# The first head's row of shifts: spread on TensorE and copied in, where a transfer carried it

## The chip, the cores and the metric

One Trainium2 chip, one of its cores. The metric is the device time of one execution, in microseconds (us), median over runs. TensorE (PE) does products, with its own queue for loading weights (PEld); VectorE (DVE) and ScalarE (ACT) do elementwise work and reductions; GpSimd (POOL) does elementwise work; SyncE (SP) issues most transfers (DMAs). Each engine works its instructions in the order in which the program lists them.

## What is computed

Attention over 4 batches x 8 heads, 768 tokens, 64 dimensions, in which a query sees only the keys of its own hash bucket (six sign bits of a projection), followed by a soft mixture of experts. Cut to what matters here:

```python
q_bits = (np.einsum('bhsd,dk->bhsk', q, proj) > 0)
k_bits = (np.einsum('bhsd,dk->bhsk', k, proj) > 0)
mask = q_bucket[:, :, :, None] == k_bucket[:, :, None, :]
scores = np.where(mask, scale * np.matmul(q, k.transpose(0, 1, 3, 2)), -1e9)
scores = scores - np.max(scores, axis=-1, keepdims=True)
attn = np.exp(scores)
attn = attn / (np.sum(attn, axis=-1, keepdims=True) + 1e-09)
x = attn @ v                     # all heads, to (3072, 512)
logits = x @ phi                 # 8 experts x 4 slots
slot_out = relu(softmax(logits, tokens).T @ x @ w1) @ w2
return softmax(logits, slots) @ slot_out
```

## The kernel before, in words

**One head.** For a head, tile Y holds in its 128 partitions the high parts of q (side 0) and k (side 1) in rows 0 to 63, one row (64) for a shift, twelve rows of sign bits scaled so that any mismatch costs a huge penalty, and low parts in rows 96 to 127; tile X holds the other parts of the split. Three pairs of X and Y go round (`XYs`, `N_Y` = 3), so that head 0 has the first pair, head 1 the second, head 2 the third. `smax` (line 463) makes approximate masked scores with rows 0 to 95 of Y, queries in the output's partitions, and VectorE takes the maximum of each query (lines 477 and 480). A head's 6 x 768 columns of maxima products lie in nine tiles of 512 columns (some products have 512, some 256), in two PSUM buffers; each tile has one reduction. `shift` (line 484) turns the maxima into the shifts of the 768 queries (three small VectorE operations, lines 489 to 492): `mz` holds in columns 0 to 5 minus the maximum of query tile t, and in columns 6 to 11 a large number for queries with no match. `shift_rows` (line 496) must lay these as a row over the 768 queries into partition 64 of side 0, the first six into X and the others into Y: TensorE transposes `mz` (line 499), ScalarE copies the 12 x 128 result to SBUF (line 502), and SyncE moves it with one transfer into the row (line 503, through `move`, line 383). `scores` (line 506) then makes the exact scores with keys in the output's partitions, two products for each piece (Y first, X second), again nine tiles of 512 columns, here in three PSUM buffers, and ScalarE takes the exponential (line 519) into `pts`. `av` (line 534, products on line 544) multiplies them with the values, `acc` (GpSimd, lines 526 and 532) sums them.

**Order.** Nothing is scheduled by a tool: `STEADY` and `ONCE` (lines 45 to 155) give each step of each head a due time, in units of one slot, `at` (line 894) looks it up, and the steps are sorted by it (line 983) and listed in that order. Steps without a line of their own take that of the steady pattern. Negative times are the start, before the steady pattern. So the tables fix the order in every engine's queue, and the times in them are ranks, not microseconds.

**The start.** Head 0 is treated apart. Its bits come from `first_bits` (products, line 437; query and key, each in two pieces, each piece in its own group of 32 output partitions), and `first_over` (line 426) compares them on VectorE straight into Y (`over`, line 409). Bits of later heads are made by `bits` (line 418, products on line 415), compared into the tile `bt`, and moved from there into Y by four transfers a head (`spread_bits`, line 453). `more_bits` (line 444) makes head 1's bits. `load_cst` (line 289) loads the identity, which `copy_ident` (line 340, on GpSimd) copies where TensorE uses it. `spin` (line 326) runs products on a tile of ones, `idle`, only to keep TensorE going; `smax` of head 0 runs one after most of its products (line 482). `idle` lies in the third X tile, and `first_rows(2)` (line 343, on GpSimd) fills that tile and the third Y tile's rows later: lines 346, 347 and 348. `load(4)` (line 258) fetches q and k of heads 4 and 5.

**Around the change** TensorE's list is, before the change: the transpose of head 0's shifts, two maxima products of head 1, `spin(2)`, four more maxima products, then the first scores of head 0, mixed with the remaining maxima of head 1; then, head 0's last scores mixed with head 2's first maxima, among them the transpose of head 1's shifts; then head 0's `av`. SyncE's list is: the row of head 0's shifts, `load(4)`, head 2's four bit transfers, the values of head 1 (`load_v`), `spread_x(1)` and `spread_l(2)`, the row of head 1's shifts.

```python
    def first_rows(i):
        ts = XYs[i] if i else Xs[0]
        if i == 2:
            nc.gpsimd.memset(Xs[2][64:96, 0].bitcast(F32), 0.0)
        nc.gpsimd.memset((ts[64:96, 1] if i == 2 else ts[64:96]).bitcast(F32), 0.0)
        nc.gpsimd.memset(ts[ROW:ROW + 1, 1].bitcast(F32), 1.0)
```

`one_rec` (line 645), near the kernel's end, already does the kind of product that the change adds: a column of a tile, broadcast to 32 columns as weights, times the identity (line 650), two columns for each of three ranges, in two groups of output partitions.

## Time and profile before

| | |
|---|---|
| median of 3 runs | 469.77 us (469.76 to 470.04) |
| the profiled execution's own time | 471.7 us |
| its span, first to last instruction | 469.8 us |
| granted TensorE clock, mean of the span | 0.998 |
| TensorE busy | 458.1 us, 98% |
| VectorE busy | 388.7 us, 83% |
| ScalarE busy | 247.9 us, 53% |
| GpSimd busy | 327.2 us, 70% |

How to read it: the profile is of one execution. Its times count from the start of the span. A row of a timeline gives start, duration, engine, line of the program, operation, output<-inputs, shapes and how many instructions were merged into the row, and in square brackets the idle time of the engine ahead of it with what ended it; "issue" is time in which the engine waited for nothing that the profile shows. A merged row's duration runs from the first start to the last end. Products are pipelined, so that one may start before the record of the one ahead has ended; TensorE's pace is read from the distance of starts, or from the chain. A product of plain float32 numbers is counted as two instructions. The chain is the work that ended last, followed back from the last instruction.

### The profile page before, as it was taken

Reading aid. Unit: us, or ns where it says so; the run is one execution under the profiler, and the core shown is the slowest. Engines: PE = TensorE matmul, PEld = TensorE weight load, DVE = VectorE, ACT = ScalarE, POOL = GpSimd, SP = SyncE. Lnnn points to the kernel's source line nnn. Section 1 sums busy time; section 2 is a strip of 40 time slices with the busy share of each in tenths; the row PEclk is TensorE's granted clock in tenths of the full one; section 3 lists DMA queues with packets and bytes.
Section 4 is the critical chain, followed back from the end, with each engine's and each line's share of the span. In section 5 each row is a group of like instructions: output and inputs, shape, how many; then the busy total and the mean of one; then the engine's idle time right before and its main releaser. Section 6 shows DMA issues by size and latency. Waiting matters only on the chain.

```text
span 469.8 us, 10650 instructions
## 1 busy us (share of the span) xinstructions
PE 458.1 (98%) x3974; PEld 289.6 (62%) x3974; DVE 388.7 (83%) x722; ACT 247.9 (53%) x469; POOL 327.2 (70%) x205
## 2 busy tenths in 40 slices
PE   8989999999999999999999999999999999999993
PEld 3556666667666666666656666666666666554472
DVE  6848898989888898989898979898888987777953
ACT  5255646464656655555555464646566546541242
POOL 7867977878785988787868988787849888910000
PEclk9999999999999999999999999999999999999999
DMA  5757578868686677868684877775756669999997
GB/s 156 182 146 176 152 159 239 170 196 193 186 203 170 136 185 178 232 173 228 165 224 136 190 220 168 231 169 171 179 187 145 197 162 299 340 355 367 411 357 315
DMA packets 39792, 99.24 MB, mean 211 GB/s; under 512 B 7471, under 2 KB 13757, under 8 KB 39741
## 3 DMA queue, kind: packets, MB, share of 16 engines
q1 hardware_dynamic: 39580, 98.17, 73.8%
q8 instruction: 31, 0.51, 0.5%
q10 hardware_dynamic: 160, 0.39, 0.4%
q14 instruction: 21, 0.16, 0.1%
HBM read 52.71 MB, written 6.29 MB: 126 GB/s over the span
## 4 chain that ended last, share of the span: by engine, by line
PE 92%; DVE 1%; issue 1%; POOL 0%; ACT 0%; DVEq 0%
PE st L515 29%; PE av L544 26%; PE smx L474 16%; PE mi L1101 3%; PE qh L1051 3%; PE mi L556 2%; PE mi L415 2%; PE mi L607 2%; PE mi L572 2%; PE mi L592 1%; PE mi L788 1%; PE mi L499 1%; PE qh L1121 1%; PE qa L1065 0%; POOL stage L379 0%
## 5 line engine op out<-in xcount | busy, mean ns | idle before, releaser
L519 ACT ACTIVATE pt<-st 128x512 f32<-128x512 f32 x288 | 164.0, 596 | 62.6 <-PE st L515 56.9
L515 PE MATMUL st<-XY 128*128 128x256 f32 (+1 forms) x768 | 177.8, 347 | 0.0
L532 POOL TENSOR_TENSOR acc<-acc,pt 128x768 f32<-128x768 f32 x85 | 155.8, 1833 | 6.5
L480 DVE TENSOR_REDUCE mx<-smx 128x1 f32<-128x512 f32 x192 | 131.0, 688 | 26.9 <-PE smx L474 24.4
L515 PEld LDWEIGHTS st<-XY 128*128 128x128 f32 x768 | 125.2, 190 | 17.6 <-ACT pt L519 1.7
L474 PE MATMUL smx<-XY 96*128 96x512 f32 (+1 forms) x384 | 119.2, 359 | 1.7 <-issue 1.3
L474 PEld LDWEIGHTS smx<-XY 96*128 96x128 f32 x384 | 66.7, 190 | 31.4 <-issue 11.5
L532 POOL TENSOR_TENSOR av<-av,pt 128x768 f32<-128x768 f32 x40 | 73.4, 1836 | 3.1
L477 DVE TENSOR_REDUCE mx<-smx 128x2 f32<-128x512 f32 x96 | 65.8, 686 | 5.2 <-PE smx L474 4.5
L544 PE MATMUL av<-pt,av 128*32 128x384 f32 x768 | 67.6, 486 | 0.0
L526 POOL TENSOR_TENSOR acc<-pt 128x768 f32<-128x768 f32 x22 | 40.4, 1838 | 37.4 <-ACT pt L519 37.4
L544 PE MATMUL av<-pt,v 128*32 128x384 f32 x768 | 65.5, 486 | 0.0
L548 ACT COPY avs<-av 128x384 f32<-128x384 f32 x32 | 15.2, 476 | 83.9 <-PE av L544 83.9
L376 DVE TENSOR_REDUCE stage<-stage 128x768 fp32r<-128x1536 f32 x28 | 49.2, 1790 | 0.0
L564 DVE RECIPROCAL dl<-sm 128x128 f32<-128x128 f32 x45 | 38.8, 916 | 12.1 <-ACT sm L559 8.3
L544 PEld LDWEIGHTS av<-pt,av 128*32 128x32 f32 x768 | 24.9, 110 | 36.8 <-issue 36.4
L544 PEld LDWEIGHTS av<-pt,v 128*32 128x32 f32 x768 | 24.9, 110 | 36.0 <-issue 35.2
L526 POOL TENSOR_TENSOR av<-pt 128x768 f32<-128x768 f32 x10 | 18.4, 1838 | 15.5 <-ACT pt L519 15.5
L369 ACT ACTIVATE stage<-stage 128x768 fp32r<-128x768 f32 x28 | 22.5, 836 | 4.4 <-DMA stage<-qk 2.1
L609 DVE TENSOR_TENSOR xq<-mi,r 128x256 f32<-128x256 f32 x45 | 17.4, 415 | 1.1 <-PE mi L607 1.1
L880 DVE STREAM_TRANSPOSE w<-call 32x256 f32<-32x256 f32 (+2 forms) x48 | 14.9, 333 | 1.6 <-PE qh L1051 1.1
L1101 PE MATMUL mi<-w 128*32 128x128 f32 (+1 forms) x336 | 15.1, 299 | 0.0
(209 smaller groups left out, 401.7 us busy)
## 6 DMA issues: line engine op xcount, KB each, us to landing
w<-w SPq DMA_DIRECT2D x51, 512.0 KB
XY<-stage SPq DMA_DIRECT2D x62, 384.0 KB
XY<-stage SPq DMA_DIRECT2D x62, 192.0 KB
stage<-qk SPq DMA_DIRECT2D x28, 384.0 KB
out<-stage SPq DMA_DIRECT2D x12, 512.0 KB
stage<-w SPq DMA_DIRECT2D x7, 512.0 KB
av<-vt SPq DMA_DIRECT2D x16, 192.0 KB
v<-vt SPq DMA_DIRECT2D x16, 192.0 KB
```

What stands on the lines that cost most here:

```text
L369: nc.scalar.activation(w[:, 2 * x], raws(h, x), AF.Copy, scale=-1.0 if h > 2 else 1.0)
L376: nc.vector.tensor_reduce(out=w[:, 2 * x + 1], in_=stage[:, x:n + 1:n - x].rearrange("p t s -> p s t"), axis=AX.X, op=ALU.add, negate=True)
L474: nc.tensor.matmul(pt[:, o:o + b - a], Ys[h % N_Y][0:96, 0, t * P:(t + 1) * P], Ys[h % N_Y][0:96, 1, a:b], start=True, stop=True)
L477: nc.vector.tensor_reduce(out=mx[:, n - 1:n + 1], in_=pt.rearrange("p (a x) -> p a x", a=2), axis=AX.X, op=ALU.max)
L480: nc.vector.reduce_max(out=mx[:, n:n + 1], in_=pt, axis=AX.X)
L515: nc.tensor.matmul(pt[:, o:o + b - a], x[:, 1, i * P:(i + 1) * P], x[:, 0, a:b], start=first, stop=not first)
L519: nc.scalar.activation(pts[i // 2][:, 512 * u:512 * u + 512], pt, AF.Exp, scale=D ** -0.5)
L526: nc.gpsimd.tensor_tensor(out=s["acc"], in0=pr[:, 0:S], in1=pr[:, S:2 * S], op=ALU.add)
L532: eng.tensor_tensor(out=s["acc"], in0=s["acc"], in1=pr[:, a * S:(a + 1) * S], op=ALU.add)
L544: nc.tensor.matmul(s["av"][D * c + d:D * c + d + 32, 0:HC], s["v"][:, i, d:d + 32], pr[:, o + c * HC:o + (c + 1) * HC], start=(i == 0), st ...
L564: nc.vector.reciprocal(out=st[h]["rs"][:, k * P:(k + 1) * P], in_=st[h]["sm"][:, k * P:(k + 1) * P])
L1101: nc.tensor.matmul(po[32 * j:32 * j + 32], hTs[g][:, f, 32 * j:32 * j + 32], wt[1, x, 2 * g + f // 4, j][f % 4][:, cols], start=(g + f == ...
```

## The change

For head 0 alone, `shift_rows` no longer transposes and moves. Instead `first_shift` multiplies each column of `mz`, broadcast to 32 columns as weights, with the identity: 12 products of 128 columns, in three ranges of columns (k) by four groups of 32 output partitions (j). After them, partition 0 of each group holds half a row (384 queries): groups 0 and 1 the halves of X's row, groups 2 and 3 those of Y's. Two copies on ScalarE (X) and two on VectorE (Y) put them into partition 64, half 1 first. Head 1 and later keep the transfer.

The due times change: in TensorE's list, two idle products (`spin(2)`) now follow the first score products, and not head 1's second maxima product; after them head 0's score products alternate with head 1's maxima from the start; all of head 0's scores and the transpose of head 1's shifts come ahead of head 2's first maxima. The list from head 0's shifts on, for each step (head, tile, part):

```
before: shift_rows 0, smax 1,1,1  1,3,1, spin 2, smax 1,0,1  1,1,0  1,5,1  1,2,0, scores 0,2,1  0,3,0,
  smax 1,2,1  1,3,0, scores 0,0,1  0,1,0, smax 1,4,1  1,5,0, scores 0,4,0, smax 1,4,0, scores 0,3,1,
  smax 1,0,0, scores 0,1,1  0,2,0, shift 1, scores 0,0,0  0,4,1, smax 2,0,0, scores 0,5,0, smax 2,0,1,
  shift_rows 1, smax 2,1,0, scores 0,5,1, smax 2,3,1, av 0
after: shift_rows 0, smax 1,1,1  1,3,1, scores 0,2,1  0,3,0, spin 2, smax 1,0,1  1,1,0, scores 0,0,1  0,1,0,
  smax 1,5,1, scores 0,4,0, smax 1,2,0, scores 0,3,1, smax 1,2,1  1,3,0, scores 0,1,1, smax 1,4,1  1,5,0,
  scores 0,2,0, smax 1,4,0, scores 0,0,0, smax 1,0,0, shift 1, scores 0,4,1  0,5,0  0,5,1, shift_rows 1,
  smax 2,0,0  2,0,1  2,1,0  2,3,1, av 0
```

`first_rows(2)`, `load(4)` and `spread_bits(2)` keep their place behind `spin(2)` in the list. Besides, head 0's bits are made and compared in halves of 384 columns, four compares and not five, all ahead of the first maxima product; and the identity's load is listed right behind head 0's values.

```diff
-    ('first_over', 0, 0, 256): -110.0, ('first_over', 0, 256, 512): -100.0, ('first_over', 0, 512, 768): -99.0,
-    ('first_over', 1, 0, 512): -111.0, ('first_over', 1, 512, 768): -109.0, ('first_rows', 0): -115.0,
+    ('first_over', 0, 0, 384): -110.0, ('first_over', 0, 384, 768): -109.0, ('first_over', 1, 0, 384): -111.0,
+    ('first_over', 1, 384, 768): -110.5, ('first_rows', 0): -115.0,
...
-    ('load_cst',): -104.0, ('load_room', 0): 183.9, ('load_room', 1): 184.93, ('load_room', 2): 184.94,
+    ('load_cst',): -112.9, ('load_room', 0): 183.9, ('load_room', 1): 184.93, ('load_room', 2): 184.94,
...
-    ('scores', 0, 0, 0): 0.919282, ('scores', 0, 0, 1): -10.094785, ('scores', 0, 1, 0): -7.0839,
-    ('scores', 0, 1, 1): 0.473768, ('scores', 0, 2, 0): 0.521698, ('scores', 0, 2, 1): -13.756044,
-    ('scores', 0, 3, 0): -13.67708, ('scores', 0, 3, 1): -1.029943, ('scores', 0, 4, 0): -4.991552,
-    ('scores', 0, 4, 1): 1.039496, ('scores', 0, 5, 0): 1.620748, ('scores', 0, 5, 1): 3.699083,
+    ('scores', 0, 0, 0): -0.7, ('scores', 0, 0, 1): -19.2, ('scores', 0, 1, 0): -19.1,
+    ('scores', 0, 1, 1): -9.0, ('scores', 0, 2, 0): -3.0, ('scores', 0, 2, 1): -29.0,
+    ('scores', 0, 3, 0): -28.9, ('scores', 0, 3, 1): -14.0, ('scores', 0, 4, 0): -17.0,
+    ('scores', 0, 4, 1): 1.039496, ('scores', 0, 5, 0): 1.3, ('scores', 0, 5, 1): 1.4,
...
-    ('shift_rows', 1): 2.323009, ('shift_rows', 2): 11.070264, ('smax', 0, 0, 0): -101.0, ('smax', 0, 0, 1): -98.0,
+    ('shift_rows', 1): 1.45, ('shift_rows', 2): 11.070264, ('smax', 0, 0, 0): -101.0, ('smax', 0, 0, 1): -98.0,
...
     def first_over(x, a, b):
-        j = 2 * x + a // 512
-        over(Ys[0][64:80, x, a:b], first_pt[x], slice(32 * j, 32 * j + 16), cols=slice(a % 512, a % 512 + b - a))
+        j = 2 * x + a // HC
+        over(Ys[0][64:80, x, a:b], first_pt[x], slice(32 * j, 32 * j + 16), cols=slice(a % HC, a % HC + b - a))
...
-        for c, (a, b) in enumerate(((0, 512), (512, S))):
+        for c, (a, b) in enumerate(((0, HC), (HC, S))):
...
         pt = s["mt"]
+        if h == 0:
+            first_shift(pt, s["mz"])
+            return
         nc.tensor.transpose(pt[:, 0:P], s["mz"], ident)
...
+    def first_shift(pt, mz):
+        for k in range(3):
+            for j in range(4):
+                nc.tensor.matmul(pt[32 * j:32 * j + 32, k * P:(k + 1) * P],
+                                 mz[:, 3 * j + k:3 * j + k + 1].broadcast_to([P, 32]), ident, start=True, stop=True)
+        row = XYs[0][ROW:ROW + 1, 0].rearrange("o y (c s) -> o (y c) s", c=2)
+        for j in (1, 0):
+            nc.scalar.copy(row[:, j], pt[32 * j:32 * j + 1, 0:HC])
+            nc.vector.tensor_copy(row[:, 2 + j], pt[64 + 32 * j:64 + 32 * j + 1, 0:HC])
...
-    for xab in ((1, 0, 512), (0, 0, 256), (1, 512, S), (0, 256, 512), (0, 512, S)):
+    for xab in ((1, 0, HC), (1, HC, S), (0, 0, HC), (0, HC, S)):
         at(first_over, *xab)
```

## Rows read from the trace of the kernel before

**Rows 1.** The page's chain that ended last, shares of the span by engine.

```profile
PE 92%; DVE 1%; issue 1%; POOL 0%; ACT 0%; DVEq 0%
```

**Rows 2.** Waits of TensorE, whole span: who waited for whom, total, times, longest.

```profile
PE smx L772 <- ACT dl L747: 0.4, 1, 0.4
```

**Rows 3.** Timeline of TensorE, 18 to 30 us.

```profile
18.81 0.30 PE L499 MATMUL mi<-ident,bt 128*128 128x128 f32 x1 [0.22 <-POOL stage L379]
19.05 0.70 PE L474 MATMUL smx<-XY 96*128 96x512 f32 x2
...
21.93 0.64 PE L515 MATMUL st<-XY 128*128 128x256 f32 x4
...
24.77 1.82 PE L515 MATMUL st<-XY 128*128 128x512 f32 x8
27.93 0.47 PE L474 MATMUL smx<-XY 96*128 96x512 f32 x1 [1.33 <-issue]
...
29.30 0.40 PE L474 MATMUL smx<-XY 96*128 96x512 f32 x1
29.63 0.85 PE L544 MATMUL av<-pt,av 128*32 128x384 f32 x8
```

**Rows 4.** Timeline of VectorE, 18 to 30 us.

```profile
18.50 0.17 DVE L492 SCALAR_TENSOR_TENSOR bt<-mi,bt 128x6 f32<-128x6 f32 x1
18.71 0.68 DVE L410 TENSOR_SCALAR bt<-mi,con 128x384 fp32r<-128x384 f32 x1
19.55 1.29 DVE L480 TENSOR_REDUCE mx<-smx 128x1 f32<-128x512 f32 x2 [0.17 <-PE smx L474]
...
24.27 1.39 DVE L480 TENSOR_REDUCE mx<-smx 128x1 f32<-128x512 f32 x2
...
28.44 0.69 DVE L480 TENSOR_REDUCE mx<-smx 128x1 f32<-128x512 f32 x1 [2.10 <-PE smx L474]
```

**Rows 5.** Timeline of all engines, 4.8 to 12 us.

```profile
4.91 2.45 PE L437 MATMUL st<-stage,pb 64*32 64x512 f32 x8
6.95 1.96 DVE L410 TENSOR_SCALAR XY<-st,con 16x512 fp32r<-16x512 f32 x3 [1.45 <-ACT XY L431]
...
7.28 1.51 PE L415 MATMUL mi<-stage,pb 128*32 128x384 f32 x8
...
8.72 0.80 PE L474 MATMUL smx<-XY 96*128 96x512 f32 x1
...
10.28 1.09 DVE L410 TENSOR_SCALAR XY<-st,con 16x256 fp32r<-16x256 f32 x2
```

**Rows 6.** Timeline of TensorE near the kernel's end, windows at 417 and 449 us.

```profile
416.75 0.85 PE L650 MATMUL st<-ident,r 128*32 128x128 f32 x12
...
448.77 0.62 PE L1101 MATMUL mi<-w 128*32 128x128 f32 x16
```

**Rows 7.** Groups by line and form: count | busy us, mean ns | idle before.

```profile
L1122 DVE COPY stage<-qh 128x512 f32<-128x512 f32 x8 | 5.3, 686 | 2.6 <-PE qh L1121 2.6
...
L594 DVE COPY r<-mi 128x12 f32<-128x12 f32 x15 | 2.4, 161 | 0.7 <-PE mi L592 0.7
...
L655 ACT COPY avs<-st 64x384 f32<-64x384 f32 x1 | 0.5, 472 | 0.2 <-PE st L650 0.2
```

**Rows 8.** The chain in order of time, 0 to 60 us: start, time, what.

```profile
24.00 0.23 PE smx L474
```

**Rows 9.** Timeline of all engines, 15 to 48 us: SyncE's transfers, GpSimd's fills.

```profile
19.43 0.82 SPq L383 DMA_DIRECT2D XY<-mr  x1
...
20.33 0.73 POOL L346 MEMSET XY<- 32x768 f32 x1 [1.52 <-issue]
...
21.01 1.37 POOL L347 MEMSET XY<- 32x1536 f32 x1
...
21.36 3.26 SPq L383 DMA_DIRECT2D XY<-bt  x4
```

**Rows 10.** Line 474's instructions, 25.5 to 29 us: ns min/median/max, first and last start.

```profile
L474 PEldq EVENT_SEMAPHORE  x3: 51/51/1677, 26.1 to 27.9; - x3
```

## The prediction

> **What bounds the kernel now.** I read the page's chain first: 92% of the span is TensorE, one product behind the other [rows 1]. So only what moves TensorE counts, and the change ends early, before the first product of head 0's probabilities with its values (line 544), which starts at 29.63 us [rows 3]; behind that the list of TensorE's waits holds nothing longer than 0.4 us [rows 2], and the change touches nothing behind it. I therefore follow the three engines to that point, before and after; the difference there is the forecast. The timeline of TensorE [rows 3] shows the transpose of head 0's shifts at 18.81, the first score at 21.93 with no idle ahead of it, the last scores of the first run from 24.77 to 26.59, then 1.33 us idle until head 2's first maxima product at 27.93. VectorE [rows 4] reduces head 1's maxima from 19.55 on, then makes its shift, and idles 2.10 us until 28.44; so the shift was ready at 26.34.
>
> **Start of the kernel.** Five compares become four. The same compare over 384 columns takes 0.68 [rows 4]. The first maxima product needs the first two now and the first three afterwards. The first compare, at 6.95 now, waits for a 512-column bit product that becomes 384 columns: four products of 384 columns take 1.51 [rows 5], so those from 4.91 on end by 6.42, and the compares start near 6.5. Three take 2.0 and two gaps of 0.04, so 8.6, plus 0.1 until TensorE starts: 8.7, and it starts at 8.72 now [rows 5]. The two compares that now stand between reductions (1.09 us, [rows 5]) go, but TensorE works at its own pace behind them, so I book nothing; if that cover is gone, up to 1.1 us comes back. Moving the identity's load earlier frees SyncE only; its user, GpSimd's copy, runs in its own order. Nothing.
>
> **The spread instead of the transfer.** Removed: a transpose (0.30), ScalarE's copy and SyncE's transfer. Added: 12 products of 128 columns, in three rounds over four column groups. Line 650 is the same form: 6 products over two groups, counted as 12 instructions (two a product), take 0.85 [rows 6], in six steps; 16 such instructions over four groups, four steps, take 0.62 [rows 6]. So a step is about 0.11 whether two or four groups are in it, and the new function has six: 0.85, from 18.81 to 19.66. Bounds: 0.30 (the transpose) and 0.93 (the four steps' 0.62 times 6/4).
>
> Copies: each has 384 elements in one partition. No row has one; I take the time to go by elements per partition. On VectorE 512 take 0.686 and 12 take 0.161 [rows 7], so 384 take 0.161 + 372 x 1.05 ns = 0.55; on ScalarE 64x384 takes 0.47. Bounds for VectorE: 0.16 (the fixed part) and 0.69. I take 0.55, nearest in size. ScalarE: 19.70 to 20.65, beside nothing. VectorE is free at 18.71 + 0.68 = 19.39, waits to 19.69, copies until 20.24 and 20.83. **Queued behind them** are head 1's nine reductions: the first starts at 20.87 and not 19.55, 1.32 later.
>
> **The new order.** Score products can now start at 20.3 (half 1 of the row) and 20.9 (half 0), not 21.93. Behind them on TensorE come the two idle products, ending at 21.75, then head 1's other maxima, each followed by two score products; the first of these also needs the first reduction's buffer, free at 20.87 + 0.69 + 0.05 = 21.61. A 512-column product takes 0.23 [rows 8], so a tile of maxima with its scores takes 0.705; two reductions back to back are 0.61 apart (1.29 less 0.69, [rows 4]). So TensorE sets the pace: six periods on, the last maxima product of head 1 starts at 21.61 + 6 x 0.705 = 25.84, its reduction runs 26.27 to 26.96, and the shift, 0.67 behind it as now (24.27 + 1.39 = 25.66 to 26.34), is ready at 27.63. TensorE meanwhile finishes the scores at 27.03, with head 0's last 768 columns of them, which today come after 27.93, and **waits** there for the shift: the second head's transpose now stands ahead of head 2's maxima. It follows the shift by 0.14 (18.67 to 18.81), so 27.78, and the next maxima product follows 0.24 behind (18.81 to 19.05): 28.02, against 27.93 now.
>
> From there the third maxima tile of head 2 must wait for the first one's reduction (two buffers): 28.02 + 0.51 + 0.69 + 0.06 = 29.28, against 29.30 now, although 0.8 us of work went ahead of it. The value products follow 0.24 later at 29.52; now it is 0.33. **Sum: 29.52 - 29.63 = -0.1 us.** The early scores fill idle time, but what they free is spent in waiting for a VectorE that the copies made late.
>
> The profiled execution took 471.7 us: the span of 469.8 and 1.9 around it. The median of the runs is 469.77; I take the 1.9 as unchanged and put the difference on the median: **469.7 us**.
>
> **Moved steps and queues.** SyncE loses the 0.82 us transfer at 19.43, so the load of heads 4 and 5 no longer stands behind the row. Head 2's four bit transfers (from 21.36, four in 3.26, [rows 9]) can start at 19.5, once their compare is done, but the third must wait for GpSimd's fills, which overwrite what the idle products read and so start behind them: 20.33 now, 21.87 then. The second fill ends 2.05 after that start (21.01 + 1.37 less 20.33), at 23.92, so the fourth transfer is issued at 24.8 and not 23.9.
>
> **Rivals.**
> (a) *Cheap spread.* If the products take 0.30 or the copies 0.16, the maxima come 0.3 to 0.6 earlier. Floor: with no wait for the shift, the transpose follows the scores at 27.03, the maxima at 27.2, the value products at 28.6: -1.0 us, 468.8. For it: TensorE's work alone allows that. Against: rows of the same form price both.
> (b) *Slower, by head 2's bits.* The weights queue stood 1.68 us at a semaphore from 26.1 to 27.8 [rows 10], 3.9 after the fourth bit transfer's issue; the row of shifts shows the other bound, at most 2.5 from its issue (19.43) to the first score (21.93). Issued at 24.8, the bits land between 27.3 and 28.7. From 27.9 on they decide, that is when a landing takes over 3.1 us; at 28.7 the maxima start at 28.8, 0.8 late, and the value products at 30.3: 470.4. Against it: the big load that lies in the way now has gone earlier.
> (c) *The transfer's latency was the bound.* First scores move from 21.93 to 20.3; if all else rides on them, the gain is 1.6 us, 468.2. Against: the first score shows no idle ahead of it. The Trainium skill, SBUF — State Buffer, The DMA setup-cost knee, says that every transfer pays some 2 us whatever its size, so that a small one taken off a chain gives that back; by it the sum would be about -2, 467.8 as an estimate. The trace agrees on the latency, but has maxima products on TensorE while it runs.
> (d) *It does nothing*: the row isn't on the chain and head 2's bits land at 27.8 as before. Then the value products start within 0.2 of today, which my forecast covers.
>
> **Chances.** Forecast with (d) 0.72, (a) 0.14, (b) 0.09, (c) 0.05. A measurement of this kernel can tell about 0.2%, 0.94 us, from no change. Over that is (c) and the far end of (a): faster 0.08. Slower by as much needs (b) beyond its bound: 0.04. Same: 0.88. The range takes the bounds of products and copies, the floor of (a) nearly, and (b): 468.9 to 470.4.
>
> **What would show it.** Right: the new function's products take about 0.85; the two VectorE copies about 0.55 each; head 1's first reduction near 20.9; the first score near 20.3; TensorE idle some 0.7 us ahead of head 1's transpose near 27.8; the value products within 0.3 of 29.63, and the same distance from there to the end. Wrong: no idle ahead of that transpose (then (a)), a semaphore wait of head 2's maxima that ends behind it (then (b)), or a gap that opens or closes behind 30 us, where I booked nothing.

## The result and the profile after

The changed kernel takes **473.27 us** in the median of 7 runs (471.32 to 474.81), the kernel before 469.77 in 7 runs beside them (469.35 to 471.01): 1.0071 times before, 95% interval 1.0047 to 1.0096. Forecast were 469.7 us and a range up to 470.4. It is slower by over 3 us, and the forecast was wrong.

The profiled execution of the changed kernel took 474.81 us, with a span of 473.0. Its chain of work that ended last, shares of the span by engine:

```profile
PE 90%; DVE 5%; DMA 1%; issue 1%; ACT 1%; SPq 0%; DVEq 0%
```

VectorE has gone from 1% to 5% of the chain, TensorE from 92% to 90% [rows 1]. The list of TensorE's waits (who waited for whom: us in total, times, longest) says where:

```profile
PE mi L415 <- DMA stage<-qk: 1.4, 1, 1.4
PE st L528 <- DVE XY L517: 1.1, 2, 0.6
PE smx L474 <- DVE mx L480: 0.5, 1, 0.5
...
PE mi L502 <- DVE bt L492: 0.4, 1, 0.4
```

Line numbers above 498 are higher than before: 502 is the transpose (499), 512 the new products, 516 and 517 the copies on ScalarE and VectorE, 528 the scores (515), 557 the products with the values (544). The first of these waits lies in the start, ahead of head 0's shift (the yardstick comes back to it); the other three lie in the first head's stage. The timeline of TensorE there, which answers to [rows 3]:

```profile
19.15 0.86 PE L512 MATMUL mi<-ident,bt 128*32 128x128 f32 x24 [0.22 <-DVE bt L492]
19.94 0.73 PE L474 MATMUL smx<-XY 96*128 96x512 f32 x2
21.19 0.50 PE L528 MATMUL st<-XY 128*128 128x256 f32 x2 [0.51 <-DVE XY L517]
22.27 0.51 PE L528 MATMUL st<-XY 128*128 128x256 f32 x2 [0.59 <-DVE XY L517]
22.62 0.64 PE L329 MATMUL av<-XY 128*128 128x512 f32 x2
...
27.55 1.10 PE L528 MATMUL st<-XY 128*128 128x256 f32 x6
29.10 0.33 PE L502 MATMUL mi<-ident,bt 128*128 128x128 f32 x1 [0.45 <-DVE bt L492]
29.31 0.71 PE L474 MATMUL smx<-XY 96*128 96x512 f32 x3
30.57 0.50 PE L474 MATMUL smx<-XY 96*128 96x512 f32 x1 [0.55 <-DVE mx L480]
31.00 0.85 PE L557 MATMUL av<-pt,av 128*32 128x384 f32 x8
```

Behind the new products TensorE waits four times: twice for the row's two halves (0.51, 0.59), once for head 1's shift (0.45), once for a buffer of head 2's maxima (0.55). The timeline of VectorE shows why (the first row is head 0's shift, on which the stages below are aligned):

```profile
18.36 0.17 DVE L489 TENSOR_REDUCE mi<-mx 128x6 f32<-128x12 f32 x1
...
19.05 0.68 DVE L410 TENSOR_SCALAR bt<-mi,con 128x384 fp32r<-128x384 f32 x1
20.57 0.56 DVE L517 CAST XY<-mi 1x384 fp32r<-1x384 f32 x1 [0.84 <-ACT XY L516]
21.66 0.56 DVE L517 CAST XY<-mi 1x384 fp32r<-1x384 f32 x1 [0.53 <-ACT XY L516]
22.25 1.29 DVE L480 TENSOR_REDUCE mx<-smx 128x1 f32<-128x512 f32 x2
```

and the timeline of ScalarE the other half of it:

```profile
20.07 0.47 ACT L516 CAST XY<-mi 1x384 fp32r<-1x384 f32 x1 [4.26 <-PE mi L512]
21.16 0.47 ACT L516 CAST XY<-mi 1x384 fp32r<-1x384 f32 x1 [0.63 <-DVE XY L517]
```

Read the brackets: each copy on VectorE waits for one on ScalarE, and ScalarE's second for VectorE's first. The four run **one after another**, from 20.07 to 22.22, and only then does VectorE begin head 1's reductions. Against the shift of head 0, the first reduction comes 3.89 us later (22.25 - 18.36). In the kernel before it was 1.54, from head 0's shift to the reduction at 19.55 in [rows 4]:

```profile
18.02 0.17 DVE L489 TENSOR_REDUCE mi<-mx 128x6 f32<-128x12 f32 x1
```

### The profile page after: what moved, and what is told of

The parts are those of the page before. It is cut to its first block, busy times and chain, and to the rows that moved or that the text cites. A ratio compares the mean times of both kernels' runs of the same rounds, so it can differ in the third digit from the quotient of the medians.

```text
span 473.0 us, 10692 instructions
## 1 busy us (share of the span) xinstructions
PE 458.2 (97%) x3997; PEld 290.0 (61%) x3997; DVE 389.9 (82%) x723; ACT 248.9 (53%) x470; POOL 327.3 (69%) x205
## 4 chain that ended last, share of the span: by engine, by line
PE 90%; DVE 5%; DMA 1%; issue 1%; ACT 1%; SPq 0%; DVEq 0%
PE av L557 26%; PE st L528 26%; PE smx L474 15%; PE mi L1114 3%; PE qh L1064 3%; PE mi L415 3%; DVE mx L480 2%; PE mi L569 2%; PE mi L585 2%; PE mi L620 2%; PE av L329 1%; DVE mx L477 1%; DMA stage<-qk 1%; PE mi L605 1%; PE mi L801 1%
## 5 line engine op out<-in xcount | busy, mean ns | idle before, releaser
L577 DVE RECIPROCAL dl<-sm 128x128 f32<-128x128 f32 x45 | 38.8, 915 | 12.1 <-ACT sm L572 9.8
L539 POOL TENSOR_TENSOR av<-pt 128x768 f32<-128x768 f32 x10 | 18.4, 1840 | 15.8 <-ACT pt L532 15.8
```

The lines of the kernel that those rows point to most:

```text
L539: nc.gpsimd.tensor_tensor(out=s["acc"], in0=pr[:, 0:S], in1=pr[:, S:2 * S], op=ALU.add)
L577: nc.vector.reciprocal(out=st[h]["rs"][:, k * P:(k + 1) * P], in_=st[h]["sm"][:, k * P:(k + 1) * P])
```

## A yardstick: the stage and the end

Single executions scatter by a us or two, whatever the kernel: head 0's shift alone starts between 15.6 and 18.4 us in the profiled executions. This goes with TensorE's clock. In the changed kernel's profile TensorE waited from 6.15 to 7.55 us for a load (the 1.4 above), the granted clock fell to 0.50 (1.2 GHz) at 8.2, TensorE then worked without a break, and at 15.0 the clock was back at 1.00 (2.4 GHz). The row of 10 to 15 us gives the length, the busy time of PE, PEld, DVE, ACT and POOL with the number of instructions, and then the granted clock:

```profile
10.00:15.00 5.00, 5.00 (x13) 2.96 (x13) 2.77 (x4) 2.72 (x5) 5.00 (x6) 0.50 0.58 123
```

A weight load of line 329 takes 0.28 to 0.29 us in that stretch and 0.19 from 15.46 on. In the first profile of the kernel before it takes 0.29 to 0.33 until 12.6 and 0.19 from 14.05 on, so that execution, too, had the lower clock in its start:

```profile
11.71 0.29 PEld L329 LDWEIGHTS av<-XY 128*128 128x128 f32 x1 [0.35 <-PE av L329]
...
14.05 0.19 PEld L329 LDWEIGHTS av<-XY 128*128 128x128 f32 x1 [0.26 <-PE av L329]
```

In the second (before_again) it takes 0.19 from 8.2 on. In seven of the 14 profiles the full clock is on record from 4.5 to 6.0 us on, and head 0's shift starts at 15.6 to 16.5; in the other seven from 10.8 to 15.0 on (in the changed kernel for the second time), and it starts at 17.1 to 18.4.

So all stages are counted from the start of head 0's shift, in the trace: to head 1's first reduction, to head 1's shift, and to the first product with the values. A last column is the distance from the end of TensorE's last product to the end of the span. "Worked out" takes only these two: (values - 10.14 + end - 7.31) over 469.8, where 10.14 and 7.31 are the means of the second and third line (for the end, of the first three). The measured ratio compares means with runs of the kernel before taken beside each kernel, and is not always the quotient of two medians given here (start_alone's 470.33 stands beside 470.09).

| kernel | reduction | shift 1 | values | end | worked out | measured ratio, 95% |
|---|---|---|---|---|---|---|
| before | 1.54 | 7.74 | 11.61 | 7.27 | | 1 |
| before_again | 1.54 | 7.92 | 10.22 | 7.28 | 1.000 | 0.9993 (0.9978 to 1.0009) |
| start_alone | 1.54 | 7.74 | 10.05 | 7.38 | 1.000 | 0.9994 (0.9974 to 1.0014) |
| after | 3.89 | 10.12 | 12.64 | 7.83 | 1.0064 | 1.0071 (1.0047 to 1.0096) |
| old_start | 3.89 | 10.13 | 12.69 | 7.84 | 1.0066 | 1.0083 (1.0053 to 1.0112) |
| two_banks | 2.92 | 9.23 | 11.75 | 7.73 | 1.0043 | 1.0054 (1.0031 to 1.0077) |
| two_banks_old_tail | 3.18 | 9.48 | 11.18 | 7.88 | 1.0034 | 1.003 (1.0009 to 1.0052) |
| values_first | 3.24 | 9.56 | 10.07 | 7.85 | 1.0010 | 1.0038 (1.0018 to 1.0058) |
| act_old_order | 2.13 | 8.32 | 10.61 | 8.00 | 1.0025 | 1.0032 (1.0016 to 1.0049) |
| vector_load | 2.22 | 8.32 | 10.69 | 7.17 | 1.0009 | 1.0001 (0.998 to 1.0021) |
| spread_for_spin | 1.29 | 7.77 | 10.07 | 7.77 | 1.0008 | 1.0011 (0.9994 to 1.0028) |
| spread_for_spin_halves | 1.29 | 7.79 | 10.09 | 8.03 | 1.0014 | 1.0014 (0.9997 to 1.0031) |
| spins_in_halves | 1.53 | 7.98 | 10.44 | 7.78 | 1.0016 | 1.0048 (1.0028 to 1.0067) |
| idle_products | 1.54 | 7.77 | 10.71 | 7.78 | 1.0022 | 1.0045 (1.0016 to 1.0074) |

Two columns say much: from the first reduction of head 1 to its shift it is 6.1 to 6.5 us in every kernel, about the pace of VectorE's nine reductions of 0.69; and the end is 7.2 to 7.4 or 7.7 to 8.0, nothing between.

One stretch is left out, from the first value product to TensorE's last product, and it scatters as much as what is counted: 432.7 to 436.6 us in the 14 profiles. It is 434.2 in the changed kernel and 434.3 in before_again, but 432.9 in the first profile of the kernel before, the one with the long stage. So the ratios "worked out" can meet the measured ones to some thousandths only. The experiments follow in the order of the argument.

## Experiments

### 1. The kernel before once more, and the start alone

before_again is the kernel before, unchanged. start_alone is the kernel before with the change's start only; old_start is the changed kernel with the start put back:

```diff
-    ('first_over', 0, 0, 256): -110.0, ('first_over', 0, 256, 512): -100.0, ('first_over', 0, 512, 768): -99.0,
-    ('first_over', 1, 0, 512): -111.0, ('first_over', 1, 512, 768): -109.0, ('first_rows', 0): -115.0,
+    ('first_over', 0, 0, 384): -110.0, ('first_over', 0, 384, 768): -109.0, ('first_over', 1, 0, 384): -111.0,
+    ('first_over', 1, 384, 768): -110.5, ('first_rows', 0): -115.0,
...
-        for c, (a, b) in enumerate(((0, 512), (512, S))):
+        for c, (a, b) in enumerate(((0, HC), (HC, S))):
...
```

Expected of before_again:

> The kernel before, once more, to see how its start differs from run to run. Theory (the start change moves the clock): every run has the mean granted clock of 0.997 to 0.998 of the first profile, spans of 469.4 to 470.2 us, and the profile has short weight loads (0.19 us) only from about 13.6 us on. Rival (chance of the run): some runs show 0.988 to 0.992, as three of the changed kernel's seven did, and spans over 471 us.

Expected of start_alone:

> The kernel before with only the start changed (halves of 384 columns, four compares ahead of the first maxima product, the identity's load moved); row transfer and order as before. Theory (the start upsets the clock): slower than before by 0.3 to 1.5 us with runs at a clock of 0.988 to 0.992. Rival (harmless): 469.8 within 0.3, clock 0.997 to 0.998.

Expected of old_start:

> The changed kernel with the first head's bits and compares, and the identity's load, as before the change; the spread and the new order stay. Theory (the start's halves of 384 columns upset the clock and cost 0.3 to 1.5 us): clock 0.997 to 0.998 in every run, head 0's last maxima reduction ends near 17.99 and not 18.32, and the time falls by 1 to 1.5 us, to about 472. Rival (the start is harmless and the loss is all from the copies): the same time as the changed kernel, 473.3 within 0.5, and the same scatter of clock.

Measured: before_again 469.74 us (0.9993), start_alone 470.33 (0.9994), old_start 474.25 (1.0083). **The start is worth nothing that these runs can tell, either way.** The fall of 1 to 1.5 us that old_start's theory expected did not come. Nor does the start upset the clock: over a whole run the mean granted clock is 0.994 to 0.998 in start_alone's 12 runs and 0.995 to 0.998 in before_again's. Three of the changed kernel's seven have 0.988 to 0.992, none of old_start's six; but single runs as low as that occur with the old start too (act_old_order 0.988, vector_load 0.988, spins_in_halves 0.991). What the second profile of the unchanged kernel brought was more: its timeline of TensorE at the end of the stage.

```profile
23.45 1.83 PE L515 MATMUL st<-XY 128*128 128x512 f32 x8
25.11 0.40 PE L474 MATMUL smx<-XY 96*128 96x512 f32 x1
25.35 0.40 PE L515 MATMUL st<-XY 128*128 128x256 f32 x2
25.59 0.28 PE L474 MATMUL smx<-XY 96*128 96x256 f32 x1
25.71 0.27 PE L499 MATMUL mi<-ident,bt 128*128 128x128 f32 x1
...
26.75 1.50 PE L544 MATMUL av<-pt,av 128*32 128x384 f32 x16
```

There is no idle behind the run of eight score products. The 1.33 us of [rows 3], which the forecast took as part of the kernel, was one late landing in one execution: head 2's maxima stood at a semaphore for head 2's bits [rows 10]. Of the fourth bit transfer, issued at 23.91, 12 of 13 pieces are reported by 25.83 and the last at 27.73; the semaphore opened at 27.76. In that execution a 16 KB packet of instructions ran from 25.70 for 0.93 us while the bits were on their way; in before_again the same packet started at 28.62, behind them. The 14 profiles bear the packet out: in the five in which it ran between this transfer's issue and its landing, that takes 2.4 to 3.8 us; in a sixth, where it ended 0.45 us ahead of the issue, 2.3; in the other eight, 1.9. No run moves the packet and nothing else, so that it is the cause is likely, but not shown. In before_again and start_alone the stage is 10.22 and 10.05 us long, not 11.61.

### 2. Two banks

The products of Y's halves go to a tile of their own, in another bank of PSUM (the memory that TensorE's products are written to), so that ScalarE and VectorE read different tiles:

```diff
-            first_shift(pt, s["mz"])
+            first_shift(pt, p_st.tile([P, 512], F32, name="st"), s["mz"])
...
-    def first_shift(pt, mz):
+    def first_shift(pt, py, mz):
...
-                nc.tensor.matmul(pt[32 * j:32 * j + 32, k * P:(k + 1) * P],
+                nc.tensor.matmul((pt if j < 2 else py)[32 * j:32 * j + 32, k * P:(k + 1) * P],
...
-            nc.vector.tensor_copy(row[:, 2 + j], pt[64 + 32 * j:64 + 32 * j + 1, 0:HC])
+            nc.vector.tensor_copy(row[:, 2 + j], py[64 + 32 * j:64 + 32 * j + 1, 0:HC])
```

> The changed kernel with the two halves of Y's row made in another PSUM tile than those of X's. Theory (the four copies ran one after the other because they read one PSUM bank from two engines): ScalarE's and VectorE's copies now run side by side, the second VectorE copy ends some 1.0 us earlier after the products than in the changed kernel (2.1 us behind their end there, about 1.1 here), head 1's first reduction and the first value product come about 1.0 us earlier, and so does the end: 472.2 us against 473.3. Rival (they write one row of one tile, and that orders them): the copies stay one after the other, no change in the time.

Measured: 472.49 us, 1.0054. The timeline of ScalarE:

```profile
18.73 0.96 ACT L516 CAST XY<-mi 1x384 fp32r<-1x384 f32 x2 [2.62 <-PE st L512]
```

and of VectorE:

```profile
17.05 0.17 DVE L489 TENSOR_REDUCE mi<-mx 128x6 f32<-128x12 f32 x1
...
18.79 1.15 DVE L517 CAST XY<-st 1x384 fp32r<-1x384 f32 x2 [0.37 <-PE st L512]
19.97 1.29 DVE L480 TENSOR_REDUCE mx<-smx 128x1 f32<-128x512 f32 x2
```

Now both engines copy side by side, 18.73 to 19.69 and 18.79 to 19.94, and the stage is 0.89 us shorter (11.75 for 12.64). So the alternation came from what the copies read in common, and the rival, the common row that they write, fell. The edit parts tile and bank together, and no run tells which of the two the program's waits go by. In the time the gain is within the intervals (1.0071 to 1.0054); it is the stage that shows it. The Trainium skill, PSUM — Partial Sum Buffer, PSUM bank collisions raise a hardware error, has the rule: accesses of different engines are guarded by semaphores per bank and quarter of the partitions, or, in the simple form, per bank. The program's waits were not the finer form: the copies' partitions 0, 32, 64 and 96 lie in four quarters, and they waited all the same. No run here tries what the finer form would allow.

### 3. The end of the order

two_banks_old_tail puts three steps of two_banks (the transpose of head 1's shifts and head 0's last two score pieces) back to the places they had before; values_first instead lets the products with the values go ahead of what waits for VectorE (lines cut to the entries that change):

```diff
-    ('scores', 0, 4, 1): 1.039496, ('scores', 0, 5, 0): 1.3, ('scores', 0, 5, 1): 1.4,
+    ('scores', 0, 4, 1): 1.039496, ('scores', 0, 5, 0): 1.620748, ('scores', 0, 5, 1): 3.699083,
...
-    ('shift_rows', 1): 1.45,
+    ('shift_rows', 1): 2.323009,
```

```diff
-    ('shift_rows', 1): 1.45,
+    ('shift_rows', 1): 3.67,
...
-    ('av', 0, 0): 4.673382,
+    ('av', 0, 0): 3.66,
...
-    ('smax', 2, 3, 1): 4.095543,
+    ('smax', 2, 3, 1): 4.89,
```

> The two-bank kernel with the transpose of head 1's shifts and head 0's last two score pieces back behind head 2's first maxima, as before the change. Theory (the transpose placed ahead makes TensorE wait for VectorE): the stretch from head 0's shift to the first value product falls from 11.75 to about 10.9 us, no wait of TensorE for VectorE's line 492 near the second shift, time 0.8 under the two-bank kernel's 472.5. Rival (the reductions' lateness alone decides, wherever the transpose stands): 11.6 to 11.8 us, no gain.

> The two-bank kernel with the first value products ahead of the transpose of head 1's shifts and of head 2's fourth maxima product, so that nothing on TensorE waits for VectorE there. Theory (the early scores do fill idle time, and what they free is lost in these waits): the stretch from head 0's shift to the first value product falls to 9.5 to 10.1 us, and the time to that of before or up to 0.7 under it. Rival (the lateness of VectorE comes out again behind the value products): the first value product comes early, but a wait opens behind the 4 us of value products, and the time stays over 471.5.

Measured: 471.34 us (1.003) and 471.7 (1.0038). With the old end the stage is 0.57 us shorter than two_banks's (11.18), though head 1's first reduction comes a little later: head 2's maxima and the last scores cover the wait for head 1's shift, which the changed order had put first. In the time this gain is not clear of the intervals. values_first, timeline of TensorE:

```profile
25.06 0.64 PE L474 MATMUL smx<-XY 96*128 96x512 f32 x3
25.63 1.50 PE L557 MATMUL av<-pt,av 128*32 128x384 f32 x16
27.06 0.33 PE L502 MATMUL mi<-ident,bt 128*128 128x128 f32 x1
...
134.06 0.47 PE L474 MATMUL smx<-XY 96*128 96x512 f32 x1 [1.44 <-DMA XY<-bt]
```

The values start 10.07 behind the shift, but their first run stretches over 12.69 us to head 1's, 0.96 longer than in all others (11.7), since the steps put off stand in it. Of the 1.1 us to two_banks_old_tail 0.14 is left. So the stage came as the theory had it and the time as the rival had it, over 471.5. A wait of 1.44 us at 134 us, for another head's bits, then costs more; act_old_order, whose order is the old one, waits 0.80 us at the same step, there for VectorE, so I don't lay it to the order.

### 4. The products and the copies apart

act_old_order is the kernel before, in its own order and with its own start, with the 12 products in the transpose's place and all four copies on ScalarE (`first_shift` as in the change, but for the last line shown):

```diff
+        if h == 0:
+            first_shift(pt, s["mz"])
+            return
...
-            nc.vector.tensor_copy(row[:, 2 + j], pt[64 + 32 * j:64 + 32 * j + 1, 0:HC])
+            nc.scalar.copy(row[:, 2 + j], pt[64 + 32 * j:64 + 32 * j + 1, 0:HC])
```

vector_load is the kernel before with four additional copies on VectorE:

```diff
         nc.scalar.copy(mr, pt[0:2 * NT, 0:P])
+        if h == 0:
+            for n in range(4):
+                nc.vector.tensor_copy(pts[2][0:2 * NT, n * P:(n + 1) * P], pt[0:2 * NT, 0:P])
```

> The kernel before with its start and its order, only the transfer of head 0's row replaced by the 12 products and four copies, all four on ScalarE, none on VectorE. Theory (what is left of the loss is VectorE's lateness and the order that waits for it): from head 0's shift to the first value product 10.1 to 10.7 us, as in the undisturbed runs of before (10.05 and 10.22) plus at most the 0.55 of the products; the time within 0.7 of before. Rival (the products and copies themselves cost): 11.5 us or more for that stretch, and 1.5 us or more over before.

> The kernel before with four more VectorE copies of 12x128 numbers from the transposed tile, behind ScalarE's, 1.1 us of VectorE work at the place where the change puts its copies; the copied numbers are overwritten and change nothing. Theory (VectorE's queue is the cost): head 1's first reduction 1.0 to 1.2 later after head 0's shift than in before (1.54), the first value product 0.8 to 1.2 later (10.1 becomes about 11.1), and the time 0.6 to 1.2 over before. Rival (VectorE has slack there, as the 2.1 us idle in the first profile of before suggested): the time within 0.3 of before.

Measured: act_old_order 471.54 us (1.0032), stage 10.61; vector_load 469.79 (1.0001), stage 10.69. Both put head 1's first reduction 0.6 to 0.7 us later (vector_load's four copies take 0.87 us, not the 1.1 expected), and both stages grow by 0.4 to 0.6: **VectorE's reductions set the stage**, and it does not matter whether VectorE itself or the products ahead of head 1's maxima hold the first one up. For act_old_order VectorE's timeline names the products' side, TensorE's maxima (compare 19.55 with 0.17 in [rows 4]):

```profile
18.53 1.29 DVE L480 TENSOR_REDUCE mx<-smx 128x1 f32<-128x512 f32 x2 [0.57 <-PE smx L474]
```

But the times differ by 0.3% where the stages are alike. vector_load's time came as its rival had it, that of the kernel before, though its interval (up to 1.0021) leaves room for the longer stage; act_old_order's is 1.8 us over the kernel before, not within the 0.7 of its theory. What differs as well is the end, 8.00 against 7.17, and in these two profiles the stretch between, 435.1 against 433.4.

### 5. The end of the span

All kernels with the spread have the longer end. They also show 32 packets in the page's queue of 16 KB instruction packets, the others 31. In the last 12 us of the span, the transfers of before_again (packets, MB, share of 16 engines):

```profile
q1 hardware_dynamic: 1050, 3.78, 79.9%
q14 instruction: 1, 0.01, 0.2%
```

and of the changed kernel:

```profile
q1 hardware_dynamic: 988, 3.58, 75.8%
q8 instruction: 1, 0.02, 0.5%
q14 instruction: 1, 0.01, 0.2%
```

The additional packet starts 8.95 us before the end, among the last transfers out. The 12 products count as 24 and replace one transpose, so TensorE's program has 23 products and 23 weight loads more. spins_in_halves lengthens it by as much without the spread: each of the 23 filler products becomes two of half the columns. idle_products does it in another way, with small products in two idle stretches:

```diff
-        for _ in range(n):
-            nc.tensor.matmul(pt[:, 0:cols], idle[:, 0:P], idle[:, P:P + cols], start=True, stop=True)
+        for k in range(2 * n):
+            nc.tensor.matmul(pt[:, 0:cols // 2], idle[:, 0:P], idle[:, P:P + cols // 2], start=True, stop=True)
```

```diff
+    def small(n):
+        pt = p_av.tile([P, 512], F32, name="av")
+        for _ in range(n):
+            nc.tensor.matmul(pt[0:32, 0:8], idle[:, 0:32], idle[:, P:P + 8], start=True, stop=True)
...
+        if x == 0:
+            small(11)
...
             spin(1)
+            if n == 3:
+                small(12)
```

> The kernel before; each of TensorE's 23 filler products is issued as two of half the columns, so TensorE's program grows by 23 products and 23 weight loads, as the spread's did, and nothing else changes. Every kernel with the spread shows 32 instruction packets on TensorE's queue where before shows 31, and its end stands 0.5 to 0.7 us further behind TensorE's last product (7.7 to 8.0 us, 7.2 to 7.4 without). Theory (the longer program brings one more instruction packet, beside the last transfers out): 32 packets, the last one in the last 10 us of the span, the distance from TensorE's last product to the end 7.7 to 8.0 us, the time +0.5 us, 1.0012 times the kernel before. Rival (the longer end comes from SyncE's program, which is one transfer shorter with the spread): 31 packets or 32, the distance 7.2 to 7.4 us, no change of the time.

> The kernel before, with 23 additional products of 8 columns on 32 weight columns, 11 of them behind the first bits (where TensorE is idle for 0.68 us until a landing) and 12 behind the fourth piece of head 0's maxima (idle for 0.71 us until VectorE). The program has as many products and loads as with the spread or with the halved fillers, and the fillers are as before. Theory (the halved fillers' 1.0048 came from the length of TensorE's program): 32 instruction packets, the distance from TensorE's last product to the end 7.7 to 8.0 us, the start of head 0's shift no more than 0.5 us later, and 1.003 to 1.005 times before. Rival (the length costs its 0.5 us at the end alone, and the rest of the halved fillers' cost lay in their being halved): the same packets and distance, and 1.000 to 1.002. If the start of head 0's shift is over 0.5 us later, that much goes off the ratio first.

Measured: spins_in_halves 471.76 us (1.0048), idle_products 471.98 (1.0045; its runs from 469.07 to 477.47, the widest of all). Both show 32 packets and an end of 7.78 us: the longer program makes the longer end, and SyncE's shorter program, the rival, does not, since it is as before in both. But in the mean both lost about 2 us, not 0.5. In idle_products the stage starts as in before_again (16.54 and 16.53), and the list of TensorE's waits has a new first place among the transfers:

```profile
PE smx L481 <- DMA XY<-bt: 1.7, 2, 1.3
```

The longer of the two, in the timeline of TensorE:

```profile
370.34 0.85 PE L524 MATMUL st<-XY 128*128 128x512 f32 x4
372.48 0.36 PE L481 MATMUL smx<-XY 96*128 96x256 f32 x1 [1.29 <-DMA XY<-bt]
```

and the transfers of the window from 369.4 to 370.9:

```profile
q1 hardware_dynamic: 90, 0.07, 23.8%
q8 instruction: 1, 0.02, 5.6%
```

A packet of instructions (from 369.49, 1.31 us long) runs while the bits are on their way again: of the last bit transfer, issued at 368.77, 12 of 13 pieces are reported by 371.31 and the last at 372.23. The other 0.4 us is in the first head's stage, with a packet from 22.52 ahead of it (28.62 in before_again). A longer program moves the packets to other work: the first starts 3.1 to 6.0 us behind head 0's shift in the ten kernels whose program is longer, and 7.7 to 12.1 behind it in the other four. 0.47 at the end, 0.57 in the stage and 0.7 here (before_again waits 0.6 us at this step, for VectorE) come to 1.7 us; 0.45% of 470.6 is 2.1. For spins_in_halves the profiled execution, 470.76 us, is faster than its median by 1.0 and shows only 0.8 us of the loss; where the rest lies stays open.

### 6. The spread without its costs

spread_for_spin is act_old_order with the products put two maxima later, in place of two filler products that it leaves out, so that they hold up nothing of head 1's first reduction. spread_for_spin_halves has in addition the remaining fillers halved:

```diff
-    ('shift', 0): -71.801989, ('shift', 1): 0.712928, ('shift', 2): 8.719961, ('shift_rows', 0): -45.474049,
+    ('shift', 0): -71.801989, ('shift', 1): 0.712928, ('shift', 2): 8.719961, ('shift_rows', 0): -27.264969,
...
-    for n in range(3):
+    for n in range(2):
         at(spin, 2, tag=n)
```

> The kernel before with the spread of the first head's row, all four copies on ScalarE, and the 12 products put two maxima later, where before has two filler products (0.62 us), which are left out. Theory (the stage ends when VectorE has made head 1's reductions, and what cost was that the products and copies delayed the first of these): first reduction of head 1 at +1.54 us from the start of head 0's shift as in the kernel before, value products at +10.1 to +10.3 us (before without the late packet 10.1 to 10.2; the same products ahead of the maxima 10.61), and what is left in the time is the longer end, +0.5 us: 1.000 to 1.0015 times before. Rival (the products cost their 0.86 us on TensorE wherever they stand): value products at +10.6 us or later and 1.003, as with the products ahead of the maxima. Third (the spread gains after all, because the scores no longer wait for the row's transfer): value products before +9.9 us, 0.999 or less.

> The kernel of the run before this one with the 21 filler products that it keeps issued as two halves each: TensorE's program is 21 products and loads longer still, so the additional instruction packet comes earlier, ahead of the last transfers out. Theory (it is the packet's place in time that costs): the packet 1 us or more earlier from the end than in the kernels with the spread so far, the distance from TensorE's last product to the end back to 7.2 to 7.5 us, and the time that of the kernel before, 0.999 to 1.0005. Rival (a longer program or SyncE's shorter one costs 0.5 us whatever the place): the distance stays at 7.7 to 8.0 us, and the time 1.001 to 1.0015.

Measured: 470.33 us (1.0011) and 470.25 (1.0014). The timeline of TensorE in spread_for_spin:

```profile
18.63 0.73 PE L474 MATMUL smx<-XY 96*128 96x512 f32 x2
19.30 0.86 PE L512 MATMUL mi<-ident,bt 128*32 128x128 f32 x24
20.15 1.10 PE L474 MATMUL smx<-XY 96*128 96x256 f32 x3
...
21.77 0.94 PE L528 MATMUL st<-XY 128*128 128x256 f32 x4
```

Head 0's shift starts at 18.12 here, head 1's first reduction at 19.41, even 0.25 us earlier than before against that shift, and the values 10.07 behind it. So the spread costs the stage nothing when VectorE is left alone. It also gains nothing: the first score comes 3.65 us behind the shift instead of 3.91 to 3.99, and the values at the same 10.1, because head 1's reductions end when they did. What is left is the longer end; both ratios' intervals include no change. Halving the fillers brought the additional packet 1.2 us earlier (10.17 us before the end), but the end stayed at 8.03: that the packet's place among the last transfers sets the end was the theory, and it fell. That a longer program has the longer end holds in all ten kernels that have it; by which step is open. No version beat the kernel before by more than its interval.

## Why the prediction was wrong, step by step

The times of the changed kernel are given less 0.34 us, by which its shift of head 0 started later (18.36 for 18.02).

- **The products: right.** Forecast 0.85 from 18.81; measured 0.86 from 18.81. The row of the same form over two groups priced them.
- **The copies' durations: right.** 0.55 and 0.47 forecast, 0.56 and 0.47 measured, although no row had one partition.
- **"ScalarE: 19.70 to 20.65, beside nothing": the step that failed first.** I priced each copy and let the two engines run side by side, without asking whether they read one tile. They took turns: VectorE was done at 21.88 and not 20.83, the first score came at 20.85 and not 20.3, head 1's first reduction started at 21.91 and not 20.87, and the transpose of head 1's shifts at 28.76 (27.78), head 2's maxima at 28.97 (28.02), the values at 30.66 (29.52). So 1.04 us went through VectorE's nine reductions to the value products, plus 0.1. two_banks gives 0.9 of it back: with the copies side by side the first reduction comes 2.92 us behind head 0's shift, for 2.85 in the forecast.
- **What waits for a late VectorE: seen, its direction right.** The idle ahead of the transpose is there (0.45 us for some 0.7 forecast), and so is the wait for head 2's first buffer (0.55). The old end of the order saves 0.57, as the old order covers the wait.
- **The baseline: the step with the largest error.** I compared 29.52 with 29.63, and the 29.63 held a wait of 1.33 us that is not in the other executions of that order (10.05 and 10.22 for 11.61). My own row of it said "issue", that is, nothing that the profile shows, and [rows 10] a semaphore; I read it as a bound of every run, even as rival (b)'s price. That the profiled execution took 471.7 us where the median was 469.77 was a sign, and I put the forecast on the median all the same. Against the usual stage my forecast of 11.50 was already 1.4 us slower than before.
- **"the same distance from there to the end", and "I booked nothing": wrong by 0.5.** The longer program of TensorE was not in the working at all.
- The start, booked at nothing: right within 0.2% (0.9994).

1.04 + 0.1 through the copies, 1.5 from the baseline (11.61 - 10.14) and 0.5 at the end are 3.1 of the 3.57 us between 469.7 and 473.27; 0.4 remains. Three of the changed kernel's seven runs had a mean granted clock of 0.988 to 0.992; the mean of the other four is 472.64 us, that of all seven 473.30. This sum sets lengths from single profiles against a difference of medians, and leaves out the stretch behind the stage, which was 1.3 us shorter in the first profile of the kernel before than in before_again. So it is an account and not a proof: two_banks shows the copies' share, before_again and start_alone that the 1.33 us are no fixed part of the kernel, and section 5 the end's.

**The rivals.** (a), a cheap spread, fell with the copies' prices. (b), head 2's bits, did not happen in the changed kernel: its waits hold none for them, since the last were issued at 25.90 and landed at 27.82, ahead of the maxima at 28.97. But the landing that it lived on is real, and TensorE waits for such bits now and then in other kernels (0.3 us in two_banks_old_tail, 1.4 in values_first, 1.7 in idle_products); I had it as a fixed part of one and not as chance. (c), the transfer's latency as the bound, fell: in spread_for_spin it is gone and the values come no earlier, and of the transfer before_again's waits show 0.2 us. The rule that I quoted from the Trainium skill, SBUF — State Buffer, The DMA setup-cost knee, holds for the transfer itself: in the kernel before the row was issued at 19.43 and its last piece reported at 21.42. But TensorE had other work meanwhile, and nothing was on the chain to be given back. (d), that nothing happens, is what spread_for_spin shows, and the kernel as changed does not.

A rival I did not have: that two engines take turns at one tile. Its price, all four copies in a row (2 x 0.55 + 2 x 0.47 = 2.04 us for 1.1), stood in my own terms.

## What to carry to other kernels

Before two engines are booked side by side, ask for each operand whether both touch one PSUM tile: if so, add their times instead of taking the longer (2.15 us here, 1.21 with two tiles). An idle stretch marked "issue" in one profile is not yet part of the kernel: take the profile of a second execution before a forecast is compared with it. And in a stage that VectorE paces, freeing a transfer bought nothing here, while holding up VectorE's first reduction by 0.6 to 0.7 us lengthened the stage by 0.4 to 0.6.

## What the chip showed that I had not expected

- Lengthening TensorE's program by 46 instructions, in idle time and without any other change, cost 0.45% (0.16% to 0.74%) in the mean. One packet of instructions more comes near the end, and the end is 0.5 us longer; the other packets, of 0.9 to 1.9 us each, move onto other transfers, and beside one of them TensorE waited 1.3 us for a landing.
- 12 float32 products of 128 columns on 32 columns of weights take 0.86 us in four column groups, as forecast from 6 in two groups (0.85): the price goes with the number of steps (six in both), not with the number of groups.
- A copy of one partition with 384 elements takes 0.56 us on VectorE and 0.47 on ScalarE, about what one takes on many partitions.
